# Fourier mixing and a leaky-ReLU layer on one core: another order of the head, with x taken in even and odd rows and zero products on TensorE

## The chip, the cores and the metric

The kernel runs on one core of a Trainium2 chip. The metric is the device time of one execution in microseconds (us); lower is better. Five runs of the kernel before took 1935.4 to 1936.79 us, with a median of 1936.24.

The core has a matrix engine (TensorE, PE in the profile, its weight loads PEld), three engines for elementwise work (VectorE or DVE, ScalarE or ACT, GpSimd or POOL) and a queue engine (SyncE or SP) that issues DMA transfers. Data lies in SBUF, products come out in PSUM, and inputs and outputs are in DRAM. Each engine takes its instructions in order.

## What is computed

```python
# x: 8 x 3008 x 256 float32
X = np.fft.fft(np.fft.fft(x, axis=1), axis=2).real.astype(np.float32)
h = X.reshape(8 * 3008, 256) @ w_in        # w_in:  256 x 2048
g = np.maximum(0.01 * h, h)
out = (g @ w_out).astype(np.float32)       # w_out: 2048 x 256
```

The real part of a two-dimensional Fourier transform of each of 8 batches is taken, and each of the 24064 rows then goes through a two-layer network with a leaky ReLU. Both weights arrive as float64, since NumPy multiplies them by a float64 scalar, and the kernel turns each into float32 itself.

## The kernel before

**Fourier part.** The 256-point transform over the features is not done on x. It is multiplied into w_in instead: `fold_w_in` (line 352) multiplies 512 columns of w_in at a time by a table of cosines and sines (`feat_sb`) into `wf`, one half of it for cosines and one for sines. What is left is the 3008-point transform over the rows. It uses symmetry: the host lays x out so that a row, its mirror row and their mirrored features meet, and the kernel adds and subtracts ("folds") them on DVE. `fold_rows` (line 235) adds mirrors and then adds and subtracts the two halves of the features, for each half h of x; `fold_halves` (line 246) adds and subtracts the two halves of x; both write into x's own tile. A row of parity 0 is folded a third time, in `fold_x_quarters`. Each batch has two units, for odd (c = 1) and even (c = 0) output rows. `dft` multiplies a unit's folded rows by sequence tables (`sequence`, lines 387 to 415), once for cosines (block 0) and once for sines (block 1): eight instructions on four tiles of even rows into one PSUM buffer (L402) and six on three tiles of odd rows into another (L412). `butterfly` (line 418) joins the two into `mix0` or `mix1`, with one ACT copy and four DVE instructions. Feature 128 (the Nyquist column, `nyx`) goes the same way for all batches at once in `nyquist`, through DRAM (`nyq_dram`) and spread over the partitions (`spread`), since only one row of products belongs to it.

**Network part.** A unit's 753 or 752 columns are cut into blocks j of 251 or fewer. The 2048 hidden values are 16 tiles of 128; a step (j, f) takes two of them. `up` (line 485) multiplies mix by wf into two PSUM buffers (L491), adds the Nyquist row times `wn` (a column of weights, L496), forms sum and difference (L500, L501) and applies the leaky ReLU on ACT (L502), giving the tile `g`. Before the change the two tiles of step f are f and f + 8. `down` (line 542) multiplies g by w_out and adds up over f in PSUM: `down_plain` for the first two blocks (L534, 16 instructions), and for all others a seven-product scheme (L554, 14 instructions) with sums of g made on POOL (L509 to L512) and sums of w_out made by `combine_w_out` (L385). The first 16 steps are the "plain" ones, alternating between the two blocks; they need w_out and w_in as they arrive. `down` of a step is written three steps after its `up` (`lag`).

**Weights.** `Weights` (line 290) loads 512 columns of float64 (0.52 MB) into one of five buffers, which have tags o (two), e (two) and raw (one) and are used in turn. `begin` (L319, L320 on DVE, L321, L322 on ACT) and `end` (L332, L333, L334 on DVE) take the bits apart and put a float32 together. There are 8 such parts in w_in and 8 in w_out. `wn` is row 0 of the sine half of wf. It lies in one partition and has to be spread over 128, so `spread_wn` (line 360) writes it to DRAM and reads it back in the other shape, both from ACT's queue.

**What sets the order.** The kernel is written with a tile framework. It places semaphores, gives out buffers (PSUM has four named "up", used by up, the transforms and the folding of w_in alike, and four named "sum"), and, unless told otherwise, chooses each engine's order itself from priorities in written order and an estimate of when each instruction can run. So the timeline of before mixes conversions, steps and folds of x freely. A transfer that is issued waits also for a transfer issued some eight before it to have landed.

Of the kernel before, what the change touches and what calls it, by code (L numbers as in the profile page):

```python
# [55 lines left out]
P = 128  # L56
# [3 lines left out]
NT = 7  # L60
# [44 lines left out]
def laid_out(x):  # L105

    m = np.concatenate([m_order(0), m_order(1)], axis=1)
    rows = 2 * m + np.repeat([0, 1], NI)  # L110
    d = np.concatenate([np.arange(P + 1), np.arange(D - 1, P, -1)])
    x = np.concatenate([x, np.zeros((B, 1, D), x.dtype)], axis=1)

    def taken(rows, d):
        return x[:, np.where(m < 0, S, rows % S)][..., d]

    mirrored = (D - d) % D
    return np.stack([
        np.stack([taken(rows, d), taken(S - rows, mirrored)], axis=2),
        np.stack([taken(H - rows, d), taken(H + rows, mirrored)], axis=2),  # L120
    ], axis=2)

# [79 lines left out]
def tile_fnet_leaky_relu(  # L202
# [24 lines left out]
    def load_x(b, q=None):  # L227
        t = xp.tile([P, 2, 2, NT, D], F32, tag="x", bufs=1, name="xt")
        for h in range(2):
            (q or nc.sync).dma_start(t[:, h], x[b, :, h])  # L230
# [4 lines left out]
    def fold_rows(t, h):  # L235


        a, z = t[:, h, 0], t[:, h, 1]
        nc.vector.tensor_tensor(a, a, z, op=ALU.add)
        lo, hi = a[:, :, 1:P], a[:, :, P + 1 : D]  # L240
        nc.vector.tensor_tensor(z[:, :, P + 1 : D], lo, hi, op=ALU.subtract)
        nc.vector.tensor_tensor(z[:, :, 1:P], lo, hi, op=ALU.add)
        nc.scalar.copy(z[:, :, 0:1], a[:, :, 0:1])
        nc.gpsimd.memset(z[:, :, P : P + 1], 0.0)

    def fold_halves(b, t):

        a, z = t[:, :, 0], t[:, :, 1]
        nc.vector.tensor_tensor(a[:, 0], z[:, 0], z[:, 1], op=ALU.add)
        nc.vector.tensor_tensor(a[:, 1], z[:, 0], z[:, 1], op=ALU.subtract)  # L250
        zs[b] = t
# [19 lines left out]

    quarters = {}
# [9 lines left out]
    wn_dram = dram.tile([2, F // 2], F32, name="wn_dram")  # L282
    tabs = {}

    def load_tab(q, n, c):
        t = const.tile([P, TW[c][n % 2]], F32, name=f"tab_{n}_{c}")
        q.dma_start(t, seq_tab[n, c, :, 0 : TW[c][n % 2]])
        tabs[n, c] = t

    class Weights:  # L290
# [7 lines left out]
        def __init__(self, src, dst):  # L298
            n = len(parts)
            tag, bufs = (("o", 2), ("e", 2), ("raw", 1))[n % 3]  # L300
            self.raw = work.tile([P, 2 * WN], F32, tag=tag, bufs=bufs, name="raw")
            self.dst = dst
            self.f64 = src.dtype != F32
            raw = self.raw if not self.f64 else self.raw.bitcast(src.dtype)
            nc.sync.dma_start(raw[:, 0 : src.shape[1] * src.shape[2]].rearrange("p (c n) -> p c n", c=src.shape[1]), src)  # L305
# [5 lines left out]
        def begin(self):  # L311
# [3 lines left out]
            self.power = work.tile([P, WN], F32, tag="power", bufs=2, name="power")  # L315
# [7 lines left out]

        def end(self):
            if not self.f64:
                nc.vector.tensor_copy(self.dst, self.raw[:, 0:WN])
                return
            hi, lo = self.word(I32, 1), self.word(U32, 0)
            man, power = self.dst, self.power
            man_i, power_i = man.bitcast(I32), power.bitcast(I32)  # L330
            v = nc.vector
            v.scalar_tensor_tensor(man, in0=lo, scalar=2.0**-32, in1=man_i, op0=ALU.mult, op1=ALU.add)  # L332
# [5 lines left out]
    def convert(made):  # L338
        for w in made:
            w.begin()  # L340
        for w in made:
            w.end()

    def load_w_in(f0):
        n, made = w_in.shape[1] // F, []
        for a in range(2):
            w = work.tile([P, WN], F32, tag="win", bufs=4, name="win")
            src = w_in[a * P : (a + 1) * P, n * f0 : n * (f0 + WN)].rearrange("p (c n) -> p c n", c=1)
# [3 lines left out]
    def fold_w_in(f0, made):  # L352

        for w in range(2):
            pt = up_ps()
            for a in range(2):
                nc.tensor.matmul(pt, lhsT=feat_sb[:, a, w * P : (w + 1) * P], rhs=made[a].dst, start=(a == 0), stop=(a == 1))  # L357
            nc.scalar.copy(wf[:, w, f0 : f0 + WN], pt)

    def spread_wn(f0):  # L360


        row = wn_dram[:, f0 : f0 + WN]
        nc.scalar.dma_start(row.rearrange("(o h) n -> o h n", o=1), wf[0:1, 1].rearrange("o (h n) -> o h n", h=2)[:, :, f0 : f0 + WN])
        at = f0 // P

        def rest():
            for h in range(2):
                nc.scalar.dma_start(wn[:, h * NH + at : h * NH + at + WN // P], row[h].rearrange("(q p) -> p q", p=P))  # L369
        return rest  # L370

    def load_w_out(f):
        made = []
        for h in range(2):
            at = (h * NH + f) * P
            src = w_out[at : at + WB * P, :].rearrange("(c p) d -> p c d", p=P)
            made.append(Weights(src, wo[:, h, f : f + WB, :].rearrange("p c d -> p (c d)")))
        return made
# [51 lines left out]
    def dft(u, blk):  # L430
# [3 lines left out]
        if c == 1:  # L434
# [15 lines left out]
    def fold_nyquist():  # L450
        nc.vector.tensor_tensor(nyb, nya, nyb, op=ALU.add)
        nc.vector.tensor_tensor(nya[:, 0], nyb[:, 0], nyb[:, 1], op=ALU.add)
        nc.vector.tensor_tensor(nya[:, 1], nyb[:, 0], nyb[:, 1], op=ALU.subtract)

    def nyquist(c):
# [8 lines left out]
        def rest():  # L464
            t = work.tile([P, UW[0]], F32, tag="mix0", bufs=2, name="nyq")
            butterfly(t, sums, B, 0, c)
            nc.sync.dma_start(nyq_dram[:, c, 0 : UW[c]], t[0:B, 0 : UW[c]])
        return rest
# [7 lines left out]


# [6 lines left out]

    def up(j, f):
        b, c, at, n, _ = blocks[j]
        pt = [up_ps("cos_ps"), up_ps("sin_ps")]
        for blk in range(2):
            for h in range(2):
                fs = slice((h * NH + f) * P, (h * NH + f + 1) * P)  # L490
                nc.tensor.matmul(pt[blk][:, h * n : (h + 1) * n], lhsT=wf[:, blk, fs],  # L491
                                 rhs=mixed[b, c][blk][:, at : at + n], start=True, stop=True)
        cos = work.tile([P, 2 * CW], F32, tag="cos", bufs=3, name="cos")
        for h in range(2):
            hs = slice(h * n, (h + 1) * n)
            nc.vector.scalar_tensor_tensor(cos[:, hs], in0=spreads[b, c][:, at : at + n],  # L496
                                           scalar=wn[:, h * NH + f : h * NH + f + 1],
# [27 lines left out]
    def down_plain(j, f):  # L525

        _, _, _, n, first = blocks[j]
        if f == 0:
            sums[j] = [ps.tile([P, 512], F32, tag="sum", bufs=4, name="sum_ps") for _ in range(2)]
        a = hidden.pop((j, f))  # L530
        for d in range(2):
            for r in range(2):
                for h in range(2):
                    nc.tensor.matmul(sums[j][d][:, r * n : (r + 1) * n], lhsT=wo[:, h, f, d * P : (d + 1) * P], rhs=a[r][h],  # L534
                                     start=(f == 0 and r == 0 and h == 0), stop=(f == NH - 1 and h == 1), skip_group_check=True)
        if f == NH - 1:
# [33 lines left out]
    def step(at):  # L570
        if at < len(steps):
# [6 lines left out]
            if n + 1 < len(units) and f == 4:  # L578
                if part == 0 and n > 0:
                    spread(units[n + 1])  # L580
                if part == 0:
                    if n % 2 == 1:
                        t = xs.pop(b + 1)
                        for h in range(2):
                            fold_rows(t, h)
                        fold_halves(b + 1, t)
                elif n > 0:
# [3 lines left out]
        if at >= lag:  # L591
# [4 lines left out]
    nc.vector.memset(inf[:, 0:1], 1151.0)  # L596
    nc.vector.memset(inf[:, 1:2], 255.0 * 2.0**23)
    w0 = load_w_in(0)
    nc.sync.dma_start(feat_sb, feat_tab.rearrange("(a p) n -> p a n", p=P))
    w2 = load_w_in(2 * WN)  # L600
    nc.sync.dma_start(nyx, x_nyq)
    t0 = load_x(0)
    for n in range(4):
        load_tab(nc.sync, n, 1)
    convert(w0)
    fold_w_in(0, w0)
    convert(w2)
    fold_w_in(2 * WN, w2)
    spread_wn(0)()
    fold_nyquist()  # L610
    fold_rows(t0, 0)
    fold_rows(t0, 1)
    fold_halves(0, t0)
    nyquist(1)()
    dft(units[0], 0)()
    spread(units[0])
    dft(units[0], 1)()
    at = 0

    def some_steps(n):  # L620
        nonlocal at
        for _ in range(n):
            step(at)
            at += 1

    o = load_w_out(0)
    convert(o)
    some_steps(plain)
    w = load_w_in(WN)
    convert(w)  # L630
    fold_w_in(WN, w)
    some_steps(plain)
    w = load_w_in(3 * WN)
    convert(w)
    fold_w_in(3 * WN, w)
    spread_wn(WN)()
    some_steps(plain)
# [47 lines left out]
```

## Time and profile before

| | before |
|---|---|
| median of 5 runs | 1936.24 us |
| the profiled execution: device time | 1936.3 us |
| its span, first to last instruction | 1934.5 us |
| PE busy | 1909.3 us (99%) |
| DVE, ACT, POOL busy | 1148.9, 468.7, 1056.3 us |
| mean granted TensorE clock | 0.996 |
| first product on PE | 10.28 us |
| first instruction of L534 | 46.26 us |
| first instruction of L554 | 146.50 us |

The page of a profile gives busy time by engine, a strip of 40 slices, and the chain of waits that ended last. Other views of the same trace are the chain in order of time, the timeline of merged instructions (in brackets the idle time of the engine before one and what ended it), and tables of busy time by stretch. A matmul on float32 is recorded as two instructions. Busy times of neighbouring instructions overlap a little, so distances from start to start are used where a sum is made.

### The profile page before, as it was taken

What the parts mean: (1) busy time and instruction counts of PE and PEld (TensorE: products, weight loads), DVE (VectorE), ACT (ScalarE), POOL (GpSimd) and SP (SyncE); (2) the same over time, 40 slices, a digit from 0 to 9 for tenths busy, and PEclk for the clock granted to TensorE, in tenths of its full rate; (3) what the DMA queues carried; (4) which work ended last, traced back from release to release, by engine and by line L of the source; (5) the groups of instructions that cost most, each with busy time, mean ns of one, the idle gap of its engine ahead of it and who ended that gap; (6) DMA issues with size and microseconds to landing.
All of it is one profiled execution on the core that took longest, in us unless ns stands there. A gap on an engine that the chain in (4) does not pass through costs nothing.

```text
span 1934.5 us, 24654 instructions
## 1 busy us (share of the span) xinstructions
PE 1909.3 (99%) x8988; PEld 1689.4 (87%) x8988; DVE 1148.9 (59%) x2245; ACT 468.7 (24%) x560; POOL 1056.3 (55%) x1508
## 2 busy tenths in 40 slices
PE   5999999999999999999999999999999999999999
PEld 3888888888888888888888888888888888888888
DVE  7975455585455845567555775457645585545554
ACT  3422222222222222222222222222222222222221
POOL 0215555575555755557555665557655575555554
PEclk8999999999999999999999999999999999999999
DMA  7220000020001000020000200002000020000000
GB/s 276 63 87 30 11 20 11 25 93 11 19 22 73 34 12 30 12 90 17 22 19 11 95 22 12 19 11 96 22 11 19 11 106 11 19 12 22 11 11 22
DMA packets 25600, 73.68 MB, mean 38 GB/s; under 512 B 4596, under 2 KB 17524, under 8 KB 23432
## 3 DMA queue, kind: packets, MB, share of 16 engines
q1 hardware_dynamic: 23360, 72.09, 10.1%
q8 instruction: 72, 1.18, 0.3%
q14 instruction: 48, 0.39, 0.1%
q10 hardware_dynamic: 2120, 0.02, 0.1%
HBM read 47.38 MB, written 24.71 MB: 37 GB/s over the span
## 4 chain that ended last, share of the span: by engine, by line
PE 98%; DMA 1%; DVE 0%; issue 0%; ACT 0%; SPq 0%; ACTq 0%; DVEq 0%
PE sum_ps L554 56%; PE cos_ps L491 17%; PE sin_ps L491 17%; PE sum_ps L534 3%; PE dft_ps L412 3%; PE dft_ps L402 2%; PE up_ps L357 1%; DMA raw<-in_w_in_dram 0%; DMA wn_dram<-wf 0%; DVE power L333 0%; DVE e L565 0%; DVE cos L496 0%; ACT g L502 0%; ACTq L369 0%; SPq L305 0%
## 5 line engine op out<-in xcount | busy, mean ns | idle before, releaser
L496 DVE SCALAR_TENSOR_TENSOR cos<-nb,wn,cos_ps 128x251 f32<-128x251 f32 (+1 forms) x768 | 330.6, 472 | 682.7 <-PE cos_ps L491 682.5
L502 ACT ACTIVATE g<-g 128x1004 f32<-128x1004 f32 (+1 forms) x384 | 399.2, 1040 | 1154.7 <-DVE g L501 1106.4
L509 POOL TENSOR_TENSOR s<-g 128x251 f32<-128x251 f32 (+1 forms) x368 | 265.8, 722 | 726.2 <-ACT g L502 721.8
L554 PE MATMUL sum_ps<-s,wt 128*128 128x251 f32 (+1 forms) x2208 | 527.8, 374 | 0.0
L554 PEld LDWEIGHTS sum_ps<-s,wt 128*128 128x128 f32 x2208 | 416.7, 189 | 52.0
L491 PE MATMUL cos_ps<-mix,wf 128*128 128x251 f32 (+1 forms) x1536 | 388.2, 375 | 0.0
L491 PE MATMUL sin_ps<-mix,wf 128*128 128x251 f32 (+1 forms) x1536 | 387.8, 375 | 0.0
L554 PE MATMUL sum_ps<-g,wo 128*128 128x251 f32 (+1 forms) x1472 | 372.6, 375 | 0.0
L491 PEld LDWEIGHTS cos_ps<-mix,wf 128*128 128x128 f32 x1536 | 291.8, 190 | 35.6 <-issue 1.8
L491 PEld LDWEIGHTS sin_ps<-mix,wf 128*128 128x128 f32 x1536 | 290.9, 189 | 34.2 <-DVE mix L427 0.2
L554 PEld LDWEIGHTS sum_ps<-g,wo 128*128 128x128 f32 x1472 | 280.1, 190 | 38.1
L512 POOL TENSOR_TENSOR s<-g,s 128x251 f32<-128x251 f32 (+1 forms) x368 | 273.7, 744 | 28.9
L500 DVE TENSOR_TENSOR g<-cos,sin_ps 128x502 f32<-128x502 f32 (+1 forms) x384 | 259.6, 676 | 47.9 <-DVE cos L496 9.8
L510 POOL TENSOR_TENSOR s<-s,g 128x251 f32<-128x251 f32 (+1 forms) x368 | 269.8, 733 | 0.0
L511 POOL TENSOR_TENSOR s<-g 128x251 f32<-128x251 f32 (+1 forms) x368 | 265.3, 721 | 0.0
L501 DVE TENSOR_TENSOR g<-cos,sin_ps 128x502 f32<-128x502 f32 (+1 forms) x384 | 257.2, 670 | 0.0
L554 PE MATMUL sum_ps<-g,wt 128*128 128x251 f32 (+1 forms) x736 | 216.0, 375 | 0.0
L554 PE MATMUL sum_ps<-s,wo 128*128 128x251 f32 (+1 forms) x736 | 216.0, 375 | 0.0
L554 PEld LDWEIGHTS sum_ps<-s,wo 128*128 128x128 f32 x736 | 139.8, 190 | 16.1
L554 PEld LDWEIGHTS sum_ps<-g,wt 128*128 128x128 f32 x736 | 140.1, 190 | 15.5
L565 DVE TENSOR_TENSOR o<-e,sum_ps 128x251 f32<-128x251 f32 (+1 forms) x184 | 67.5, 408 | 8.7 <-ACT e L563 8.7
L534 PE MATMUL sum_ps<-g,wo 128*128 128x251 f32 x256 | 58.8, 383 | 2.9 <-ACT g L502 2.9
(65 smaller groups left out, 651.8 us busy)
## 6 DMA issues: line engine op xcount, KB each, us to landing
xt<-in_x_dram SPq DMA_DIRECT2D x16, 1792.0 KB, 7.0
out_dram<-o SPq DMA_DIRECT2D x80, 251.0 KB, 2.3
raw<-in_w_in_dram SPq DMA_DIRECT2D x8, 512.0 KB, 5.3
raw<-in_w_out_dram SPq DMA_DIRECT2D x8, 512.0 KB, 4.2
out_dram<-o SPq DMA_DIRECT2D x16, 250.0 KB, 2.4
nb<-nyq_dram SPq DMA_DIRECT2D x8, 376.5 KB, 3.4
nb<-nyq_dram SPq DMA_DIRECT2D x8, 376.0 KB, 4.4
tab<-in_seq_tab_dram SPq DMA_DIRECT2D x2, 564.0 KB, 13.9
```

What stands on the lines that cost most here:

```text
L491: nc.tensor.matmul(pt[blk][:, h * n : (h + 1) * n], lhsT=wf[:, blk, fs], rhs=mixed[b, c][blk][:, at : at + n], start=True, stop=True)
L496: nc.vector.scalar_tensor_tensor(cos[:, hs], in0=spreads[b, c][:, at : at + n], scalar=wn[:, h * NH + f : h * NH + f + 1], in1=pt[0][:, hs ...
L500: nc.vector.tensor_tensor(g[:, 0], cos[:, 0 : 2 * n], pt[1][:, 0 : 2 * n], op=ALU.add)
L501: nc.vector.tensor_tensor(g[:, 1], cos[:, 0 : 2 * n], pt[1][:, 0 : 2 * n], op=ALU.subtract)
L502: nc.scalar.activation(g, g, ACT.Lrelu)
L509: nc.gpsimd.tensor_tensor(s1, a[1][0], a[1][1], op=ALU.add)
L510: nc.gpsimd.tensor_tensor(s2, s1, a[0][0], op=ALU.subtract)
L511: nc.gpsimd.tensor_tensor(s3, a[0][0], a[1][0], op=ALU.subtract)
L512: nc.gpsimd.tensor_tensor(s4, a[0][1], s2, op=ALU.subtract)
L534: nc.tensor.matmul(sums[j][d][:, r * n : (r + 1) * n], lhsT=wo[:, h, f, d * P : (d + 1) * P], rhs=a[r][h], start=(f == 0 and r == 0 and h ...
L554: nc.tensor.matmul(sums[j][p], lhsT=still[p], rhs=moving[p], start=(f == 0 and i % 2 == 0), stop=(f == NH - 1), skip_group_check=True)
L565: nc.vector.tensor_tensor(to, x, y, op=ALU.add)
```

## The change

All of it lies before step 16, apart from small things that follow from it.

- **x in even and odd rows.** Batch 0 is loaded in four transfers, even rows first, and folded in pieces: `add_mirrors`, then `fold_columns` by feature half, then `fold_halves` by feature half and parity. Only what unit (0, 1) needs is folded at first; the differences of block 0 go to a tile of their own. The pieces for the other parity come at steps 14 and 15. The host writes the Nyquist column of x as zero and hands it over separately, so no ACT copy is needed.
- **Less weight before the first step.** w_in is taken in parts of 256, 256, 512, 512 and 512 columns, of which one 256 is folded before the first step (before: 512 twice), and in written order a part is begun (`begin`) while the part before it is ended (`convert_on`). w_out is loaded in the order 0 to 7. Step f uses hidden tiles 2f and 2f + 1 in the plain steps.
- **wn in one hop.** `spread_wn` moves 128 values at a time straight from one partition of SBUF to 128, in SP's queue; `fold_w_in` does the sine half first.
- **The first Nyquist row is spread by TensorE** (`spread_first`: a product with a row of ones, and an ACT copy), not through DRAM. The folds of the Nyquist rows move from DVE to POOL.
- **Zero products.** `keep_warm` multiplies a tile of zeros, 256 columns at a time, ten, seven and three times. The ACT function table is loaded at the start.
- **Fixed order.** Up to step 16, DVE, PE and SP take their instructions in written order, and POOL until the first unit is transformed. ACT stays planned. `down` is written two steps after `up` there. Unit 1's transforms move from the plain steps to block 2's steps 2 and 5.

```diff
+    def add_mirrors(t, h, rows):
+        a, z = t[:, h, 0, rows], t[:, h, 1, rows]
         nc.vector.tensor_tensor(a, a, z, op=ALU.add)
...
+    def fold_columns(t, h, part, rows):
+        a, z = t[:, h, 0, rows], t[:, h, 1, rows]
+        if part == 0:
+            nc.vector.tensor_tensor(z[:, :, 0:P], a[:, :, 0:P], a[:, :, P:D], op=ALU.add)
+        else:
+            nc.vector.tensor_tensor(z[:, :, P + 1 : D], a[:, :, 1:P], a[:, :, P + 1 : D], op=ALU.subtract)
+            nc.gpsimd.memset(z[:, :, P : P + 1], 0.0)
+
+    def fold_halves(t, part, c, rows, to=None):
+        i, cols = (c + part) % 2, slice(part * P, (part + 1) * P)
+        z = t[:, :, 1, rows, cols]
+        to = t[:, i, 0, rows, cols] if to is None else to[:, rows]
+        nc.vector.tensor_tensor(to, z[:, 0], z[:, 1], op=(ALU.add, ALU.subtract)[i])
...
+    RAW = "o e raw o e o e raw raw o e raw o e raw o e raw".split()
...
+    def convert_on(old, new):
+        old.mantissa()
+        if new is not None:
+            new.begin()
+        old.end()
...
+            if w == 1:
+                spread_wn(f0, n)
+
+    def spread_wn(f0, n):
+        for q in range(f0 // P, (f0 + n) // P):
+            nc.sync.dma_start(wn[:, q : q + 1], wf[0:1, 1, q * P : (q + 1) * P])
...
+    def spread_first(rows):
...
+            nc.tensor.matmul(pt, lhsT=one, rhs=rows[0:1, half], start=True, stop=True)
+            nc.scalar.copy(t[:, half], pt)
...
+    def keep_warm(n):
+        pt = ps.tile([P, 512], F32, tag="sum", bufs=4, name="sum_ps")
         for _ in range(n):
+            nc.tensor.matmul(pt[:, 0 : 2 * P], lhsT=blank[:, 0:P], rhs=blank, start=True, stop=True)
+
+    with tc.manual_schedule(engines={mybir.EngineType.DVE, mybir.EngineType.PE, mybir.EngineType.SP}):
+        with tc.manual_schedule(engines={mybir.EngineType.Pool}):
...
+            w = load_w_in(0, half)
+            load_rows(0, evens)
+            nc.sync.dma_start(feat_sb, feat_tab.rearrange("(a p) n -> p a n", p=P))
+            load_rows(1, evens)
+            nc.sync.dma_start(nyx, x_nyq)
+            for n in range(2):
+                load_tab(nc.sync, n, 1)
+            for h in range(2):
+                load_rows(h, odds)
+            for n in range(2, 4):
+                load_tab(nc.sync, n, 1)
+            o = load_w_out(0)
+            keep_warm(10)
+            fold_nyquist()
+            convert_w_in(0, half, w)
+            w, w1 = load_w_in(half, half), load_w_in(WN, WN)
+            keep_warm(7)
...
+            nyq = nyquist(1)
+            for rows in (evens, odds):
+                for h in range(2):
+                    add_mirrors(t, h, rows)
+                    fold_columns(t, h, 0, rows)
+                    if rows == odds and h == 0:
+                        fold_columns(t, h, 1, slice(0, NT))
+                fold_halves(t, 0, 1, rows, differences)
+            fold_columns(t, 1, 1, slice(0, NT))
+            fold_halves(t, 1, 1, slice(0, NT))
...
+            ready = [nyq, dft(units[0], 0), dft(units[0], 1)]
+            spread_first(ready[0]())
+            ready[1]()
+            o.begin()
+            o.mantissa()
+            ready[2]()
+
+        w[0].begin()
+        up(*steps[0])
+        o.end()
+        o1 = load_w_out(1)
+        for n in range(4):
+            load_tab(nc.sync, n, 0)
+        up(*steps[1])
+        keep_warm(3)
+        down(*steps[0])
+        convert_on(w[0], w[1])
+        convert_on(w[1], o1)
+        down_plain(*steps[1], halves=(0,))
+        fold_w_in(half, half, w)
+        convert_on(o1, w1[0])
+        o2, o3, w2 = load_w_out(2), load_w_out(3), load_w_in(2 * WN, WN, (0,))
+        w1[0].mantissa()
+        up(*steps[2])
+        down_plain(*steps[1], halves=(1,))
+        w1[1].begin()
+        up(*steps[3])
+        down(*steps[2])
+        w1[0].end()
+        convert_on(w1[1], o2)
+        down_plain(*steps[3], halves=(0,))
+        fold_w_in(WN, WN, w1)
+        convert_on(o2, o3)
...
+        up(*steps[4])
+        convert_on(o3, w2[0])
+        down_plain(*steps[3], halves=(1,))
...
+        for at, old, new in ((8, o4, o5), (9, o5, w3[0]), (10, w3[0], w3[1]), (11, w3[1], o6), (12, o6, o7), (13, o7, None), (14, None, None), (15, None, None)):
...
+            up(*steps[at])
+            down(*steps[at - 2])
+            if at > 13:
+                fold_halves(t, at - 14, 0, slice(0, NT))
```

## The prediction

> **What bounds the kernel now.** I read the page first, for shares. TensorE (PE) is busy 99% and only the first of 40 slices, 48 us each, falls short of 9 tenths:
>
> ```profile
> PE   5999999999999999999999999999999999999999
> DVE  7975455585455845567555775457645585545554
> PEclk8999999999999999999999999999999999999999
> ```
>
> So nothing outside the head (the time before step 16) can be won unless PE gets less to do, and the change leaves PE's real products as they are. Second view, the chain of waits in order of time, for the head; its columns are start, duration, engine and line:
>
> ```profile
> 2.10 5.86 DMA raw<-in_w_in_dram
> 10.28 9.70 PE up_ps L357 x16
> 20.61 4.59 DMA wn_dram<-wf
> 26.24 0.31 ACT e L423
> 26.55 4.33 issue
> 30.88 2.85 PE dft_ps L402 x8
> 33.73 3.05 PE dft_ps L412 x6
> 45.16 1.05 ACT g L502
> 46.26 8.27 PE sum_ps L534 x30
> 141.41 3.40 PE sum_ps L534 x16
> 146.50 2.96 PE sum_ps L554 x14
> ```
>
> From 46.26 on PE never waits. The full-speed price of a product half (each float product is recorded as two instructions) is 3.40 / 16 = 0.2125 us for 251 columns, so 0.43 for the 512 of L357, 0.317 for 376 and 0.159 for 188. The work done when the first L554 starts (146.50) is 32 x 0.43 = 13.7 for L357, 256 x 0.2125 = 54.4 for L534, 20 steps of up x 8 x 0.2125 = 34.0, three transforms of parity 1 at 8 x 0.159 + 6 x 0.317 = 3.17 each = 9.5, and 6.4 for those of parity 0 (0.76 + 1.28, 0.86 + 1.30, 0.86 + 1.30 in the chain). Sum 118.0. **PE has lost 146.5 - 118.0 = 28.5 us**: 10.28 before its first product, 2.8 because L357's 16 took 9.70 and not 6.86, 7.65 idle from 23.23 to 30.88, 2.7 because both transforms together took 9.08 and not 6.35, 2.86 idle before 46.26, 1.9 because the 30 there took 8.27 and not 6.38.
>
> Third, the timeline of the head, for what ended the 7.65: the "issue" hides it.
>
> ```profile
> 20.61 1.15 ACTq L364 DMA_DIRECT2D wn_dram<-wf  x1
> 26.24 0.30 ACT L423 COPY e<-dft_ps 8x188 f32<-8x188 f32 x1 [3.45 <-issue]
> 26.57 0.34 DVE L424 TENSOR_TENSOR ev<-e,dft_ps 8x188 f32<-8x188 f32 x1 [1.91 <-ACT e L423]
> 28.77 2.01 DVE L250 TENSOR_TENSOR xt<-xt 128x1792 f32<-128x1792 f32 x1
> ```
>
> VectorE (DVE) folds the whole x, and the transform starts as L250 ends, at 30.8. Within that, ScalarE (ACT) stood 5.6 us with the second hop of wn waiting in its queue, and DVE lost 1.91 behind it. Fourth, busy time by stretch: the clock, and DVE beside a full PE (columns: stretch, its length, PE, PEld, DVE, ACT, POOL, clock, DMA).
>
> ```profile
> 24.00:26.00 2.00, 0.00 (x0) 0.00 (x0) 0.67 (x1) 0.00 (x0) 0.00 (x0) 0.92 0.36 130
> 46.00:47.00 1.00, 0.74 (x2) 0.66 (x3) 1.00 (x3) 0.20 (x1) 0.00 (x0) 0.58 0.68 268
> 49.00:50.00 1.00, 1.00 (x5) 0.88 (x4) 1.00 (x4) 1.00 (x3) 0.00 (x0) 0.71 0.00 0
> 60.00:70.00 10.00, 10.00 (x41) 7.38 (x40) 9.97 (x22) 6.04 (x8) 0.00 (x0) 1.00 0.29 95
> ```
>
> The clock falls to half about 2.5 us after the last product of 23.23 and 2.8 us after that of 43.40, and returns some 3.4 us after work resumes. From 60 to 70 both PE and DVE are full.
>
> **The change, step by step.** I put the new instructions in their written order on each engine, each starting when its engine and its inputs are free. Prices are start-to-start distances in the timeline: converting 512 columns 0.34 + 0.33 + 3 x 0.60 = 2.5 on DVE, for 256 columns 1.4 (between L241, 889 columns in 1.07, and L451, 112 in 0.27, a column costs 1.0 ns and an instruction 0.16); DVE in one up 2.0; a butterfly 1.5. PE: up 1.7, down 3.4, folding 512 columns of w_in 3.4. The loads fit "3.4 us plus bytes at 0.40 MB per us" (L319 first ran at 4.70 after 0.52 MB, again at 7.99 after 1.83).
>
> *Until the first step.* Weights of 0.52 MB land at 4.7, even rows of x at 7.3 and 10.6, tables 0 and 1 at 11.8 and 13.3, odd rows at 15.2 and 17.2, tables 2 and 3 at 19.6, w_out 0 at 20.9. PE: ten zero products at first (free, PE has nothing), w_in's first 256 columns at 8.2 (their table lands at 8.0), seven zero products, the Nyquist transform 12.9 to 16.1, the even rows of block 0 to 17.4. DVE has the even rows folded by 12.9; the odd ones cost 0.87 + 0.47 + 1.0 after 15.2 and 0.87 + 0.47 + 0.47 after that: 19.4. So PE idles 2.0, then ends block 0 at 21.3. DVE goes on: 1.0 + 1.0 for block 1 (21.4), the Nyquist butterfly (22.9), block 0's (24.5), two of w_out's five conversions (25.8), block 1's (27.3). Block 1's products run from 22.0 to 25.2, as they take the PSUM buffers that the Nyquist butterfly gives up; the two products that spread the first Nyquist row end at 26.5 (new, 4 x 0.317 = 1.3). Up 0 ends at 28.3, its g at 30.8; down 0 starts at 31.2, after up 1 and three zero products. It was 46.26.
>
> *Steps 0 to 5.* Here DVE sets the pace. The quarter after, w_in 256 to 511, is converted by 37.1 (w_out 1 can only be loaded into the one "raw" buffer after w_out 0 is done at 31.0, and lands 4.2 later by the page's median); PE waits 0.8, folds to 38.8, waits 0.4 for ACT's copy. Its wn row goes in one hop from 38.4. A hop from SBUF to SBUF is not in the trace: the nearest rows, the second hop of before (2.2, median 4.4, at most 5.4 to landing), bound it from above, and 0 from below. I take 2.2, since the queue is empty then: 41.3, and g of step 2 at 44.1, when PE has just done up 3 (44.3). At 5.4, PE stands 3 us more. Then down 2 and half of down 3 to 49.4, w_in 512 to 1023 to 52.8, 0.6 for the copy: 53.4. Real work done by then: 6.8 + 9.5 + 4 x 1.7 + 3.5 x 3.4 = 35.0. Lost 18.4.
>
> *Steps 6 to 15.* Per step DVE has 2.0 + 2.5 and PE 5.1, so PE is full; g of step 5 is ready at 60.7 and wanted at 65.3. Two more folds of w_in each show a copy of 0.6. **Lost in all 18.4 + 1.2 = 19.6, against 28.5: 8.9 us won.**
>
> *Edits at nothing.* Two fold_halves (1.0 each on DVE) move to steps 14 and 15, where nothing is converted; uncovered, 2.0. The POOL fold of the Nyquist rows (three instructions under 0.4 by L385's 0.72 for 256 columns) lies under the load of the tables. The zero column of x comes with x, and an ACT copy goes (L243, 0.20): never on the path. combine_w_out, 16 x 0.72 on POOL, stays free to run before step 16. Later batches fold with 12.1 on DVE for 12.3, beside a full PE. The 16 wn issues (0.4 each) now stand in SP's fixed queue among the loads: behind each are the next weights, and an issue that waits for a raw buffer holds up the next wn row. Pairing hidden blocks 2f and 2f+1 makes the columns due in the order in which they load.
>
> *The clock.* In the ledger PE's longest pause after the start is 2.0 us, under the 2.5 seen. I charge half of one cold spell (3.4 us at half speed cost 1.7): 0.9. That zero products hold the clock is in no row: if they don't, 2.7 + 1.9 of cold work comes back at most; if they do, 0.
>
> The Trainium skill (TensorE: Matmul & The Clock Gate, Part 1) says that the clock falls after an idle window of about 3.4 us, free-running. This trace has it 2.5 and 2.8 us after the last product, so pauses are dearer than that page has them. By the page no pause of the ledger costs anything, which would give 1927.4.
>
> The profiled execution took 1936.3 with a span of 1934.5, and the runs' median is 1936.24, the same within 0.1. 1936.3 - 8.9 + 0.9 = **1928.3**.
>
> **Rivals.**
> - *Half of it is eaten, 1932.* The order is now fixed on DVE, PE and SP, while ACT stays planned; one ACT instruction in a bad place costs what L423 did (3.4 idle), or wn lands in 5.4 (3 us), or a cold spell or two (1.7 each). Speaks for it: DVE is 9.97 of 10 us busy from 60 to 70, so a late DVE finds no slack. Against: from step 6 g is 4.6 us early. 1928.3 + 3.4 = 1931.7.
> - *Slower.* One mechanism: the loads through the single "raw" buffer (w_out 1, w_out 2, a part each of w_in 1024 and 1536, w_out 7) start only when the last conversion there ends, and SP's order holds wn and the next loads behind them. If all five were exposed with 0.4 + 5.3 (the page's w_in landing) it would be 28 us: 1928 + 28 = 1956. It decides from 8 us exposed, 1.6 per load. Against: after the first, the ledger has each landing 2 to 4 us before its turn.
> - *It does not do what it says:* if the fold of x is what holds block 1, as before, and the zero products change no clock, the start of down 0 moves only by the conversion of w_in's columns 1024 to 1535 that no longer stands ahead of it (2 x 2.5 = 5.0) and DVE's 1.9: 6.9 less the new 1.3 and three pauses for copies (1.8) is 3.8, 1932.5, near no change.
>
> **Chances.** The ledger 0.58, better than it by over 4 us 0.04, half eaten or not doing what it says 0.24 (a third of it still beyond 0.2%), slower mechanism 0.14 (0.02 of it within). 0.2%, 3.9 us, is about what a measurement of this kernel can tell from no change. Faster 0.58 + 0.04 + 0.08 = 0.70, same 0.16 + 0.02 = 0.18, slower 0.12. The range leaves out the 0.04 below and the 0.12 above: low is 1928.3 less the 0.9 of the clock and 4 of the 5.0 us of pauses in the ledger (2.0, 0.8, 0.4 and three of 0.6), 1923.5; high, 1937.5, is just past no change.
>
> **What the profile will show.** The first down_plain product at about 31 and not 46; the transforms' 14 instructions at 3.2 us each time (a cold clock shows 5.9); no DRAM hop of wn and no ACT pause at the first e copy; PE without pauses beyond 0.6 from 54 on; first L554 near 138.5 (146.5 less 8.0). Wrong if PE still shows pauses over 2 us past 50, if DVE waits on raw loads, or if PE pauses after step 16.

## The result and the profile after

| | before | after | forecast |
|---|---|---|---|
| median | 1936.37 us (46 runs, 1935.25 to 1937.42) | 1932.96 us (26 runs, 1930.7 to 1934.36) | 1928.3 |
| profiled execution, its span | 1936.3, 1934.5 us | 1932.82, 1930.7 us | |
| first product of the first `down_plain` | 46.26 us | 33.84 us | 31.2 |
| first seven-product instruction | 146.34 us | 138.94 us | 138.5 |
| PE busy | 1909.3 us | 1919.2 us (zero products with it) | |

The ratio is 0.9981 [0.9976, 0.9987]: faster by 3.4 us, not by 8. The sign was right and the time lies in the range, but less than half of the forecast gain is there. Of all executions one, of run 11, took 3404.93 us at a mean granted clock of 0.556; that run's ratio leaves it out, and the other ten have a median of 1933.2. In the timelines, the first down starts 12.4 us earlier, and the first seven-product instruction only 7.4 earlier; the second number still flatters, because one transform of parity 0 (2.17 us) was done by then in the kernel before and is to come in the changed one. (146.34 is the start in the timeline; the chain has 146.50.)

The page of the changed kernel, the strip of 40 slices; the first slice of PE, 5 before, is 9 now, since PE starts earlier and zero products count as busy.

```profile
PE   9999999999999999999999999999999999999999
DVE  7868555584555755567555775558655585555554
PEclk9999999999999999999999999999999999999999
```

The chain of waits of the changed kernel in order of time (start, duration, what):

```profile
5.27 10.71 DMA xt<-in_x_dram
16.01 0.97 DVE xt L241
...
20.75 3.60 PE dft_ps L441 x6
24.35 1.28 PE dft_ps L431 x8
25.63 1.90 PE dft_ps L441 x6
27.53 1.47 PE dft_ps L516 x4
...
30.14 0.88 DVE cos L543 x2
...
33.01 0.03 DVE wo L362
...
51.98 3.45 PE up_ps L393 x8
```

Two things are to be read. The 7.7 us in which PE stood behind DVE and ACT are gone, and the head hangs on the landing of x's odd rows (16.0), then on DVE's folds (to 20.75), then on PE (to 29.0), then, through a copy on ACT, on DVE again: the products of the first step, and L362, which ends the conversion of w_out's first part at 33.70, 0.14 before the first down. And the first six products, odd rows of block 0, took 3.60 where the next six of the same shape took 1.90: a cold clock. Busy time by stretch (stretch, length, PE, PEld, DVE, ACT, POOL, clock, DMA) shows it:

```profile
20.00:20.30 0.30, 0.00 (x0) 0.00 (x0) 0.27 (x2) 0.00 (x0) 0.00 (x0) 1.00 1.04 376
20.30:21.00 0.70, 0.25 (x1) 0.28 (x2) 0.70 (x2) 0.00 (x0) 0.00 (x0) 0.51 1.07 416
23.00:23.70 0.70, 0.70 (x2) 0.41 (x2) 0.60 (x3) 0.00 (x0) 0.00 (x0) 0.50 0.71 287
23.70:24.00 0.30, 0.30 (x2) 0.15 (x2) 0.30 (x2) 0.00 (x0) 0.00 (x0) 0.97 0.10 41
```

What PE waited for in the whole span (total, times, longest):

```profile
PE cos_ps L538 <- ACT wf L394: 2.6, 4, 0.7
PE dft_ps L441 <- DVE differences L257: 1.9, 1, 1.9
PE sum_ps L650 <- POOL blank L655: 1.1, 1, 1.1
PE sum_ps L601 <- DVE o L612: 0.8, 1, 0.8
PE up_ps L393 <- DMA feat_sb<-in_feat_tab_dram: 0.7, 1, 0.7
```

Four pauses stand for ACT's copy behind a folding of w_in, one for DVE's folds of the odd rows (after it the clock is low), one each for the zeros themselves and for a table at the start, and one after step 16, where the ledger had none. The timeline of PE around the pause for the odd rows and the one after step 16:

```profile
20.75 3.60 PE L441 MATMUL dft_ps<-tab,differences 128*128 128x376 f32 x6 [1.94 <-DVE differences L257]
...
177.44 1.01 PE L538 MATMUL sin_ps<-mix,wf 128*128 128x251 f32 x4
179.20 1.11 PE L601 MATMUL sum_ps<-g,wo 128*128 128x251 f32 x4 [0.76 <-DVE o L612]
...
182.59 1.01 PE L538 MATMUL cos_ps<-mix,wf 128*128 128x251 f32 x4
```

**The ledger against the trace.** Each stretch of the profiled execution beside what the prediction's sum had for it:

| stretch | ledger | measured | difference |
|---|---|---|---|
| to the first down (L581) | 31.2 | 33.84 | +2.6 |
| from there to the first L601 | 104.1 (146.34 - 8.9 - 31.2 - 2.17) | 105.1 | +1.0 |
| from there to the start of the last L601 group | 1785.3 (1783.12 before, + 2.17) | 1786.85 | +1.6 |
| from there to the end of the span | 5.0 | 4.9 | -0.1 |
| outside the span | 1.8 | 2.1 | +0.3 |
| charged for the clock at large | 0.9 | in the rows above | -0.9 |

The last L601 group is that of the timeline's last row.

The differences add up to 4.5, which is 1932.82 - 1928.3. So no single large thing went wrong; small terms add up. The experiments ask whether each of them is really paid at the end.

### The profile page after: what moved, and what is told of

Same layout as the page of the kernel before. It is cut to its first block, busy times and chain, and to the rows that moved or that the text cites. A ratio compares the mean times of both kernels' runs of the same rounds, so it can differ in the third digit from the quotient of the medians.

```text
span 1930.7 us, 24800 instructions
## 1 busy us (share of the span) xinstructions
PE 1919.2 (99%) x9040; PEld 1696.7 (88%) x9040; DVE 1157.6 (60%) x2273; ACT 468.6 (24%) x552; POOL 1060.6 (55%) x1513
## 4 chain that ended last, share of the span: by engine, by line
PE 95%; DVE 3%; DMA 1%; issue 1%; ACT 0%; SPq 0%; DVEq 0%; ACTq 0%
PE sum_ps L601 55%; PE cos_ps L538 16%; PE sin_ps L538 16%; PE dft_ps L441 3%; PE sum_ps L581 3%; PE dft_ps L431 2%; DMA xt<-in_x_dram 1%; PE up_ps L393 1%; DVE cos L543 0%; DVE g L547 0%; DVE xt L241 0%; DVE g L548 0%; DVE xt L257 0%; DVE xt L247 0%; DVE xt L249 0%
## 5 line engine op out<-in xcount | busy, mean ns | idle before, releaser
L601 PE MATMUL sum_ps<-s,wt 128*128 128x251 f32 (+1 forms) x2208 | 528.2, 374 | 0.0
L601 PEld LDWEIGHTS sum_ps<-s,wt 128*128 128x128 f32 x2208 | 416.2, 189 | 52.6 <-issue 0.7
L601 PE MATMUL sum_ps<-g,wo 128*128 128x251 f32 (+1 forms) x1472 | 372.2, 375 | 0.9 <-DVE o L612 0.8
L601 PEld LDWEIGHTS sum_ps<-g,wo 128*128 128x128 f32 x1472 | 279.7, 190 | 40.0 <-DVE o L612 1.7
L557 POOL TENSOR_TENSOR s<-s,g 128x251 f32<-128x251 f32 (+1 forms) x368 | 276.9, 753 | 0.0
L601 PE MATMUL sum_ps<-s,wo 128*128 128x251 f32 (+1 forms) x736 | 216.0, 375 | 0.0
L601 PE MATMUL sum_ps<-g,wt 128*128 128x251 f32 (+1 forms) x736 | 216.0, 375 | 0.0
L601 PEld LDWEIGHTS sum_ps<-s,wo 128*128 128x128 f32 x736 | 139.8, 190 | 16.0
L601 PEld LDWEIGHTS sum_ps<-g,wt 128*128 128x128 f32 x736 | 140.1, 190 | 15.5
L612 DVE TENSOR_TENSOR o<-e,sum_ps 128x251 f32<-128x251 f32 (+1 forms) x184 | 67.5, 408 | 8.7 <-ACT e L610 8.7
L581 PE MATMUL sum_ps<-g,wo 128*128 128x251 f32 x256 | 57.1, 375 | 0.0
```

The source lines that it names most:

```text
L557: nc.gpsimd.tensor_tensor(s2, s1, a[0][0], op=ALU.subtract)
L601: nc.tensor.matmul(sums[j][p], lhsT=still[p], rhs=moving[p], start=(f == 0 and i % 2 == 0), stop=(f == NH - 1), skip_group_check=True)
L612: nc.vector.tensor_tensor(to, x, y, op=ALU.add)
```

## The experiments

Theory 1: the head is bound as the ledger says, PE is full from there to the end, and so every pause of PE in the head comes off the whole time when it is mended. The named ones are the cold spell, ACT's copies, and the later load of x. Theory 2, the rival, has the gain eaten elsewhere: by the fixed order, or by slack that gives back whatever the head gains. All kernels were timed in five rounds against the kernel before.

**1. zeros_between.** Four zero products between the even and the odd rows of block 0.

```diff
...
-            ready = [nyq, dft(units[0], 0), dft(units[0], 1)]
+            ready = [nyq, dft(units[0], 0, lambda: keep_warm(4)), dft(units[0], 1)]
```

> The changed kernel with four more zero products between the even and the odd rows of the first transform, where TensorE idled 1.94 us (18.8 to 20.75) and the clock then stood at half until 23.6. Theory 1, the cold spell is only part of the delay, since VectorE, not TensorE, sets the start of step 0 (its fold of x ends at 22.7 and its butterflies at 28.9, without a pause of its own): the odd rows take 1.9 instead of 3.6 us, but only about 0.9 us of it reaches the end (ratio to before 0.9977). Theory 2, the cold spell is the whole delay of the head against the ledger: 2.6 us less (0.9968). Theory 3, zero products do not hold the clock: odd rows still 3.6 us, no gain.

1931.59 us, 0.9974 [0.9963, 0.9985]. PE's timeline in this kernel has the pause covered and the clock full; the first down starts at 33.03, not 33.84.

```profile
18.55 1.89 PE L652 MATMUL sum_ps<-blank 128*128 128x256 f32 x8
20.64 2.13 PE L443 MATMUL dft_ps<-tab,differences 128*128 128x376 f32 x6 [0.20 <-DVE differences L257]
```

The 0.8 in the trace is about what theory 1 asks: 0.7 of it is the cold spell, and 0.1 that the odd rows were there earlier (15.90 and not 16.01). The interval overlaps that of the changed kernel, so the median alone would not show it.

**2. copies_covered.** The folding of w_in 1024 to 1535 does the cosine half first, and that of 1536 to 2047 stands one down earlier, right behind the up of step 11, so that PE has work while ACT copies.

```diff
...
-        fold_w_in(2 * WN, WN, w2)
+        fold_w_in(2 * WN, WN, w2, (0, 1))
...
+            if at == 11:
+                fold_w_in(3 * WN, WN, w3)
             down(*steps[at - 2])
```

> The changed kernel, but the fold of w_in for columns 1536 to 2047 stands one down earlier, and the fold for columns 1024 to 1535 makes its cosine half first, so that ScalarE's copy of what up needs first lies beside products. Theory 1, each of the four pauses behind a fold costs the 0.67 us shown and 0.26 more for the first products after it (1.11 instead of 0.85 us for four): two of them go, 1.8 us less (ratio to before 0.9972). Theory 2, VectorE is the bound there and TensorE waits for g instead: no gain, with new waits of L581 for the leaky ReLU.

1930.51 us, 0.9971 [0.9960, 0.9982]. PE's waits:

```profile
PE dft_ps L441 <- DVE differences L257: 2.2, 1, 2.2
PE cos_ps L538 <- ACT wf L394: 1.3, 2, 0.7
```

Two of the four copies are hidden. A copy costs more than its pause: in the chain the four products after it take 1.11 and not 0.85, in this kernel as in the changed one. The trace shows what the two were worth: from the first down to the first L601 it takes 103.30, and 105.10 to 105.12 in the changed kernel and in four others with the same steps there, 1.8 less. Theory 1.

**3. unit1_early.** The transforms of unit 1 go to steps 0 and 2 of block 2, so that x's buffer is free sooner.

```diff
-            if n == 0 and f in (2, 5):
-                dft(units[1], f // 5)()
+            if n == 0 and f in (0, 2):
+                dft(units[1], f // 2)()
```

> The changed kernel with unit 1's two transforms at block 2's steps 0 and 2 instead of 2 and 5. Theory 1: the second transform, ending at 150.6, is what holds x's only buffer, so x of batch 1 is loaded at 150.6 (109.2 before) and its 12 us fold runs on VectorE from 158 to 183, where TensorE waits 0.76 us for the sums of block 2; moved earlier by 5 to 10 us, that wait goes: 0.8 us less (ratio 0.9977), up to 1.4 if all that was lost after step 16 has this cause. Theory 2: the wait comes from the order of VectorE's instructions and not from the load: same time.

1931.77 us, 0.9976 [0.9966, 0.9986]. SP issues the next batch's x at 135.62 and 139.97, where the changed kernel does it at 150.65 and the kernel before did at 109.23, and the wait of L601 for DVE's L612 is gone:

```profile
176.81 1.01 PE L538 MATMUL sin_ps<-mix,wf 128*128 128x251 f32 x4
...
180.62 1.01 PE L538 MATMUL cos_ps<-mix,wf 128*128 128x251 f32 x4
```

From the sine products of that step to the next step's products it takes 3.81 here and 5.15 in the changed kernel, so the wait of 0.76 costs 1.34. The missing wait alone would prove little, since some executions of the late load do not list it either (run 9). But all nine traces with the load as late as in the changed kernel lose something there (4.15 to 5.15), and runs 3, 8 and 10, with the earlier one, nothing (3.81 or 3.82). Theory 1, at the upper end of its size by the first trace. In this profile the pause before the odd rows was 1.94 again, and yet the clock did not fall; the first down starts at 33.21.

**4. no_zeros.** All `keep_warm` calls are taken out.

> The changed kernel without any of its twenty zero products. Theory 1: the products up to 24 us run at half clock (w_in's 8 in 3.4 us, the first transform's odd rows at 3.6 as now), but VectorE sets the start of step 0, so it costs 0 to 2 us (ratio 0.998 to 0.999). Theory 2: the clock is what the head hangs on: 4 us or more slower (ratio over 1.000).

1931.32 us, 0.9974 [0.9964, 0.9984], no slower than with them. PE's timeline:

```profile
9.90 3.75 PE L393 MATMUL up_ps<-win,feat_sb 128*128 128x256 f32 x8 [9.90 <-DMA feat_sb<-in_feat_tab_dram]
...
21.54 2.13 PE L441 MATMUL dft_ps<-tab,differences 128*128 128x376 f32 x6 [0.60 <-DVE differences L257]
...
33.92 1.30 PE L581 MATMUL sum_ps<-g,wo 128*128 128x251 f32 x5 [1.27 <-DVE wo L362]
```

The zeros do hold the clock: the first eight products take 3.75 without them and 1.97 with them. But here cold work costs nothing, because DVE is what PE waits for: PE without zeros reaches the odd rows later, its pause there is 0.60 and not 1.94, and the clock holds. In front of the first down it waits for DVE's conversion of w_out (L362), in place of three zero products. The odd rows came 0.8 later here (16.80), and the first down only 0.1 later than in the changed kernel.

**5. planned_order.** The fixed order is taken off all engines; the written order is only a priority again.

> The changed kernel without the fixed order: all engines are planned, as before the change; everything else stays, zero products too. Theory 1, the fixed order is what makes the smaller pieces pay: the planner mixes conversions and folds ahead of the first unit, the first L581 comes some 5 us later and the gain over before is gone or turned (ratio 0.999 to 1.003). Theory 2, the pieces do it alone: within 0.0005 of the changed kernel's 0.9981.

1933.77 us, 0.9986 [0.9977, 0.9995]. PE waits 5.1 us for the differences, as the planner puts other work of DVE first, the clock is at half from 24.15 to 30.97, and the first down starts at 39.65, 5.8 later. The first L601 is at 141.53, only 2.6 later, and the median 0.8 to 1.2 over the changed kernel's two. The late first down is theory 1's, the ratio just within what theory 2 allowed; neither had both. PE's waits say what made up the rest:

```profile
PE dft_ps L441 <- DVE differences L257: 5.1, 1, 5.1
...
PE sum_ps L581 <- ACT g L549: 0.8, 2, 0.6
```

There is no line for ACT's copy: the planner lays products of steps between the two halves of each folding, and none of the four copies shows. The fixed order wins the start and pays for the copies, which it need not (run 2).

**6. whole_x.** x in two whole transfers and no split in rows.

> The changed kernel with x of batch 0 loaded in two whole halves and folded without splitting into even and odd rows, in the same fixed order otherwise. Theory 1, what VectorE does after the last rows have landed is what counts, and with whole halves the last rows land earlier than the odd rows do now (15.3 for 18.0 by bytes ahead of them), so the fold of x ends at about the same 22.7, while the tables land later and the transforms bunch behind them: 0 to 1.5 us slower (ratio 0.9981 to 0.9989). Theory 2, the even rows started early are what the gain comes from: 3 us slower (ratio 0.9997).

1932.79 us, 0.9982 [0.9973, 0.9990], which is not to be told from the changed kernel. In the trace the first down comes at 34.99: 1.15 later than in the first profile of the changed kernel and 1.7 later than in the second one (run 9), and the span is 0.3 and 1.6 longer. What the odd and even rows are worth lies below what these medians can tell.

**7. before_one_hop.** The kernel before with one part of the change: wn in one hop in SP's queue.

```diff
-        nc.scalar.dma_start(row.rearrange("(o h) n -> o h n", o=1), ...)
...
+                for q in range(h * NH + f0 // P, h * NH + (f0 + WN) // P):
+                    nc.sync.dma_start(wn[:, q : q + 1], wf[0:1, 1, q * P : (q + 1) * P])
```

> The kernel before, with this one part of the change: wn goes straight from one partition to 128, sixteen transfers from SyncE's queue, not through DRAM from ScalarE's. Theory 1: the 5.6 us in which ScalarE's queue stood, and the 1.91 us that VectorE lost behind it, are on the path to the first unit: 1.9 us less (ratio 0.9990). Theory 2: the gap is filled by other work anyway, or the transfers on SyncE's queue hold weights up: same or slower.

1937.11 us, 1.0004 [0.9995, 1.0013]. PE's waits in this kernel and, below, in the kernel before:

```profile
PE dft_ps L398 <- issue: 5.7, 1, 5.7
PE sum_ps L530 <- ACT g L498: 4.9, 1, 4.9
```

```profile
PE dft_ps L402 <- issue: 7.7, 1, 7.7
PE sum_ps L534 <- ACT g L502: 2.9, 1, 2.9
```

The transform gains 2.0, and the wait for g grows by 2.0: the first down starts at 46.16 and not 46.26. DVE had put folds and conversions of w_out ahead of the step, and SP issued w_out's load at 24.09 and not 18.21, behind eight hops. Theory 2 holds for this part alone.

**8. three_mended.** Edits 1, 2 and 3 together.

> The changed kernel with all three mends: zero products between even and odd rows, the two folds of w_in with covered copies, unit 1's transforms earlier. If each of the three causes is its own stretch of the path, the gains add: 0.9 + 1.8 + 0.8 = 3.5 us less than the changed kernel (ratio to before 0.9963). If VectorE bounds steps 0 to 12, the first two give nothing and it is 0.8 less (0.9977).

1928.33 us (1927.75 to 1929.94), 0.9958 [0.9946, 0.9971], whose interval lies wholly below the changed kernel's. It is the fastest version of the study. PE's waits:

```profile
PE cos_ps L540 <- ACT wf L394: 1.3, 2, 0.7
...
PE dft_ps L443 <- DVE differences L257: 0.2, 1, 0.2
```

The wait of step 16 on is gone, two copies are gone, the pause is 0.2, and the first down starts at 32.47. Against the changed kernel's medians, 1932.96 and 1932.53 (run 9), this is 4.6 and 4.2 less; the ratio's interval is 2.4 us wide to either side. The two profiled spans differ by 5.1, and the traces say where: 0.7 for the cold spell, 1.8 for two copies, 1.3 at the wait for L612, so 3.8 where the three edits aim; 0.7 because the odd rows were there at 15.35 and not 16.01, and 0.6 for a delay near 1117 us that comes and goes, are no merit of theirs. That it equals the forecast number is chance, since its first down is still 1.3 later than the ledger's.

**9. changed_again.** The changed kernel once more, unaltered.

> The changed kernel once more, unaltered, for its spread and for the profile of another execution. Its first profile had a cold spell at 20.6 to 23.6 us (0.6 us of the head, by the first L581 at 33.84 against 33.21 in a run of the same head without one) and a wait of 0.76 us at 179 (1.4 us by the time from the first L601 to the end, against 1785.4 in three other kernels). Theory 1, both come and go from one execution to the next: runs between 1930.7 and 1934.4 again, median near 1932.9, and if this profile lacks one of the two it is that much shorter. Theory 2, both belong to the program: the same two in the profile, and a span of 1930.7.

1932.53 us, 0.9980 [0.9971, 0.9989]; this profiled execution took 1931.49, 1.3 less than the first one.

```profile
20.91 2.13 PE L441 MATMUL dft_ps<-tab,differences 128*128 128x376 f32 x6 [1.93 <-DVE differences L257]
...
33.30 1.94 PE L581 MATMUL sum_ps<-g,wo 128*128 128x251 f32 x8
```

The same pause of 1.93, and no cold spell; nor is there a wait for L612 in the list, though PE still loses 0.56 in that place (4.37 and not 3.81). The 1.3 between the two spans is 0.54 at the first down and 0.8 there. So the cold spell comes and goes from execution to execution, and the size of the loss behind step 16 changes.

**10. mended_no_zeros.** three_mended without any zero products.

> The kernel with the three mends, but without any zero product (the four between even and odd rows too). Theory 1: without zeros the early products run cold, end later and so leave no long pause, and step 0 hangs on VectorE either way: 0 to 0.9 us slower than with them (1928.3; ratio to before 0.9958 to 0.9963). Theory 2, zero products between the rows are what the mends won: 2 us or more slower (0.9968).

1928.39 us, 0.9960 [0.9946, 0.9973]: 0.06 from three_mended. The time is theory 1's, its reason was not: the pause was 2.45 and not short, and the odd rows ran cold (3.63). The first down still started at 32.88, when DVE's L362 ended: 17.87 after the odd rows were there, where run 8 has 17.12, but they were there 0.34 earlier (15.01). So a cold spell that zero products prevent is worth some 0.7 in a trace, and nothing that these medians could tell.

**11. odd_rows_first.** The loads of x's odd rows are put ahead of tables 0 and 1.

> The changed kernel with the odd rows of x loaded ahead of tables 0 and 1 instead of behind them. Theory 1, the landing of the last rows sets the fold of x and so the head: they land 2.4 us earlier (0.96 MB at 0.40 MB per us), the fold ends near 20.8 instead of 22.8, but the transforms wait for the tables until 18 and run one behind the other to 28: first L581 within 1 us of 33.2. Theory 2, the fold alone decides: first L581 2 us earlier, ratio 0.997.

1933.81 us, 0.9985 [0.9976, 0.9994]. The rows landed earlier, but DVE was not through with the even ones until 15.95, and its fold of x ended at 22.66, as before (22.7). PE's timeline:

```profile
16.94 1.58 PE L431 MATMUL dft_ps<-tab,nyx 95*8 95x188 f32 x8 [2.49 <-issue]
18.32 3.65 PE L441 MATMUL dft_ps<-tab,nyx 128*8 128x376 f32 x6
```

The Nyquist transform now waited for its tables, ran cold, and the first down came at 34.82. Theory 2 falls, and theory 1, which had the first down within 1 us of 33.2, missed the size too: the earlier landing buys nothing, and the tables are late instead.

**12. two_hops.** The changed kernel with wn through DRAM in two hops, from ACT's queue.

```diff
...
-            nc.sync.dma_start(wn[:, q : q + 1], wf[0:1, 1, q * P : (q + 1) * P])
+        nc.scalar.dma_start(wn_dram[:, f0 : f0 + n], wf[0:1, 1, f0 : f0 + n])
+        nc.scalar.dma_start(wn[:, f0 // P : (f0 + n) // P], wn_dram[0, f0 : f0 + n].rearrange("(q p) -> p q", p=P))
```

> The changed kernel with this part alone undone: wn goes through DRAM in two hops from ScalarE's queue, after each fold of w_in. Theory 1, the second hop holds ScalarE's queue until the first has landed (4.6 us in the kernel before), and in the changed order the copies, power and leaky ReLU behind it are wanted at once: 2 to 5 us slower (ratio 0.9991 to 1.001). Theory 2, as in the kernel before, where one hop alone changed nothing (1.0004), the queue has time: within 1 us of the changed kernel.

1941.83 us, 1.0027 [1.0017, 1.0037]: 9.3 more than changed_again and slower than the kernel before. Its chain in order of time:

```profile
39.76 1.09 DMA wn_dram<-wf
...
40.88 5.08 DMA wn<-wn_dram
...
58.84 4.20 DMA wn_dram<-wf
```

and what DVE waited for:

```profile
DVE cos L544 <- DMA wn<-wn_dram: 19.0, 4, 7.7
```

With loads of w_out, half a megabyte each, issued at 40.38 and 57.38, a hop lasted 5.08 and 4.20; the second hop at 63.11 took 2.11. That they slowed each other is likely, not tested. DVE takes its work in a fixed order, stands at the first instruction that reads wn, and all conversions stand behind it; PE waits 5.7 for g as a result, and after a pause of 2.98 the clock is at half from 50.62 to 54.04. The direction was theory 1's; the size, 9 and not a few us, was neither's. So the one hop gains nothing in the kernel before (run 7), and without it the change would be a loss.

## Why the prediction was right in sign and short in size

- **What bounds the kernel** held: after 140 us PE is busy in every slice, and all but the loss behind step 16 (below) is decided in the head.
- **The chain that was to go** went: no pause for ACT's e copy, no 7.7 us, no DRAM hop on the path; the first down 12.4 us earlier.
- **The hop of wn**, taken as 2.2 between 0 and 5.4 us, took 1.9 to 9.7 to land with a median of 2.1. The 9.7 are the first two, queued behind the loads, before anything needs them.
- **Steps 0 to 5** took what the ledger said in sum: from the first down to the up after the second fold of w_in 56.09 - 33.84 = 22.25, in the ledger 53.4 - 31.2 = 22.2.
- **The step that failed is the sum "until the first step", 31.2.** The first down came at 33.84, and at 33.30 without a cold spell. It starts 0.14 or 0.15 us after DVE ends L362 in the changed kernel, run 9 and runs 1, 3, 4, 8 and 10, with zero products in front of it or without, so DVE's chain sets it. The ledger has that end at 31.0 ("w_out 0 is done at 31.0"). DVE's timeline in run 9:

```profile
16.16 0.96 DVE L241 TENSOR_TENSOR xt<-xt 128x768 f32<-128x768 f32 x1 [0.40 <-DMA xt<-in_x_dram]
...
22.87 0.33 DVE L453 TENSOR_TENSOR ev<-e,dft_ps 8x188 f32<-8x188 f32 x1
...
29.00 0.29 DVE L343 TENSOR_SCALAR win<-raw 128x256 int32<-128x256 int32 x1
...
32.46 0.69 DVE L362 SCALAR_TENSOR_TENSOR wo<-wo,power 128x512 f32<-128x512 f32 x1
```

  In place of "the odd ones cost 0.87 + 0.47 + 1.0 after 15.2", the odd rows were there at 16.16 (+1.0). From there to the end of L362 DVE took 17.0, in the ledger 31.0 - 15.2 = 15.8 (+1.2): 0.5 more to the end of x's folds (6.7 for 6.2), 0.2 more to the end of the butterflies, 0.5 more from there. The first profile of the changed kernel had the rows at 16.01 and a cold spell, behind which DVE stood 0.79 before it could go on with the first step's products, so 17.7. No run changed these terms one by one, but the rows were there at other times in other executions, and the first down followed: 17.12 to 17.14 behind them in runs 1, 3, 4, 8 and 9, for rows there at 15.35 to 16.80. Run 11 shows that an earlier landing alone does not help, as DVE reaches the odd rows only at 15.95.
- **ACT's copies** were in the ledger at 0.4 and three times 0.6. They were 0.61, 0.68, 0.67 and 0.68, and 0.26 more for the products that restart after each. Up to 56.09 that is made good by a wait of 0.8 for DVE that did not come; the restart there and the last two copies, 0.26 + 2 x (0.68 + 0.26) - 2 x 0.6 = 0.9, are nearly the whole +1.0. Run 2 confirms the price: 1.8 for two of them.
- **"Edits at nothing"** left one out. Moving unit 1's transforms frees x's buffer later, batch 1 is loaded at 150.65 and not 109.23, and DVE folds it among the steps from 158 to 183. In the first profile that costs PE 1.34, a wait of 0.76 and a slower restart; run 3 takes it away. Another 0.60 is lost in the same way near 1117.5 (4.41 for 3.81). It is in eight of the twelve traces with the change, not in runs 1, 4, 8 and 10 nor in the kernel before, and its cause stays open. The two make 1.9; the kernel before loses 0.4 elsewhere in this stretch (1783.12, and 1782.75 in run 8), which leaves the +1.6.
- **The clock.** The ledger took pauses under 2.5 us as safe; the 1.94 at 18.8 was not in the first profile, and was in run 9 and, just as long, in runs 3 and 12. It was charged with 0.9 and cost 0.7 in the first down. The reading that the clock "returns some 3.4 us after work resumes" holds for 46.26 only (full again at 49.58); after 30.88 it was at half until 35.93, 5.0 us. "If the zero products hold the clock, 0" was right for the wrong reason: they do hold it, yet run 10 has the same time without them, and in run 4 the pause that they lengthen is mostly gone.
- **The rivals.** The time is that of "half of it is eaten", but by a mix of small terms; of the things named there only a cold spell came, and cost 0.7. The slower mechanism, loads through the one raw buffer, did not come: DVE's only listed wait for raw is the 2.9 before the first conversion. "It does not do what it says" fell with the first down at 33.84.

On the clock, the trace of the changed kernel had 1.00 until 20.30, 1.5 us after the last product (17.28 + 1.54 = 18.82), then 0.5 until about 23.7, 3.4 us; in the second execution the clock was 1.00 throughout a like pause. The other traces' spells at half clock in the head have that length too (3.41 in runs 2, 6, 10, 11 and 12) or a multiple of it (6.83 in run 5, 10.24 in the kernel before). The Trainium skill (TensorE: Matmul & The Clock Gate, Part 1) has a free-running window of about 3.4 us: the length of the spell and its coming and going agree with that, but its rule that the clock falls after an idle window of that length does not fit a fall within a pause of 1.94.

## What to carry to other kernels

When the engine that ends the head is full from there on, a ledger of small pauses is worth making to the tenth of a us, restart included: three edits of a few lines took 4.2 to 4.6 us off the median here, more than the whole change (3.4). Ask first which engine sets the end of the head: here it was DVE, and its 17 us from the last rows on were put 1.2 too low in the ledger, in many small parts. Work that only fills an engine's waiting time gains nothing while that engine waits for another one. A fixed order makes each late transfer dear: with wn in two hops the same program lost 9 us, as everything behind the waiting instruction stood still.

## What the runs showed of the hardware

- Products of zeros count as activity for the clock: eight products after them took 1.97 us, and 3.75 without them.
- The clock can fall 1.5 us after the last product, and in another execution of the same program, with the same pause (1.94 and 1.93), does not fall at all.
- A pause of 0.67 us at a full clock costs PE about 0.9: hiding two of them took 1.8 us off the stretch (run 2).
- POOL's first addition on 128 x 112 took 1.16 us.
